# Half of one weight load moved from ScalarE's queue to SyncE's, in a GEGLU feed-forward kernel

## The chip, the core and the metric

The kernel runs on one core of a Trainium2 chip. The core has five engines with their own instruction streams: TensorE (PE, matrix products; its weight loads are listed as PEld), VectorE (DVE), ScalarE (ACT), GpSimd (POOL) and SyncE (SP). Loads and stores are issued by an engine into its queue, and all queues share the core's 16 DMA engines. The metric is device time in microseconds (us): the median of several runs. A profile is one execution, and has a time of its own.

## The reference

```python
def _gelu(x):
    return jax.nn.gelu(x, approximate=True)

# B, S, D, F = 32, 32, 1024, 3584; all inputs bf16
def reference(x, w_gate, w_up, w_down):
    return (_gelu(x @ w_gate) * (x @ w_up)) @ w_down
```

x is 1024 tokens by D = 1024; w_gate and w_up are 1024 by 3584, w_down is 3584 by 1024.

## The kernel before

Each of the two stages of products is computed as a 2x2 block product with seven multiplications instead of eight, at the price of sums of blocks on VectorE, GpSimd and ScalarE.

In the first stage the left matrix is made of w_gate and w_up: for each of the 28 blocks of 128 columns of F (block i), a11 and a12 are the first and second half of D of w_gate's columns, a21 and a22 those of w_up's. The right matrix is x transposed: B11 and B21 are the first and second half of D for tokens 0 to 511, B12 and B22 the same for tokens 512 to 1023. A half of D is four slices of 128 (KH = 4), so one product of two blocks is four matmuls of 128x128 by 128x512. The first product is a11 by B11, the second a12 by B21, added in the same PSUM bank; the fourth to seventh and the third use sums (S1 to S4 of weights, T1 to T4 of x), which are kept in a 4-byte type.

The order of the program is written out by hand. Its start is this. SyncE loads B11 with a transposing DMA (L131) while TensorE runs ten matmuls on constants (L137). ScalarE waits for the second of them and then issues w_gate's tiles (L141 to L145): a tile holds two blocks (256 columns, all of D, 512 KB), and its first half is what a11 reads, its second half what a12 reads. They are issued in this order: tile 0's first half in two pieces of 128 KB, the first halves of tiles 1, 2 and 3 (256 KB each), tile 0's second half. After the ninth constant matmul ScalarE writes a few values into B21 (L147), and this write holds back SyncE's second transposing load, B21 (L149); this is "x's second half". Behind it on SyncE's queue follow the second half of tile 2 (L150), w_up's first 256 columns (L151), the second half of tile 3 (L152), tile 4 (L153), the transposing load of the whole other half of the tokens, xt1 (L154), tile 5 in two halves (L155, L156) and w_up's next 256 columns (L157). Tiles 4 and 5 live in a part of the buffer gT that is not needed yet, so the profile calls them gT. Every load of w_gate is issued by line 86, every load of w_up by line 93, so that in the profile they carry those lines.

TensorE computes the first products of blocks 0 and 1 interleaved (L279), then those of blocks 2 to 7 (L282), then the second products of blocks 0 to 7 (L284), then both products of blocks 8 and 9 (tile 4), the first product of block 10 (tile 5), and from there the products with sums. All their matmuls are on line 195. ScalarE evicts each first product (L212) and applies the GELU to each finished gate block (L219). After the first products of blocks 0 and 1 have been evicted, ScalarE issues the second half of tile 1 (L280).

VectorE's first sums wait for w_up's first load; its T sums (L166) wait for xt1. From about 35 us on the loop runs over the remaining blocks, loading w_gate and w_up a few blocks ahead. The second stage (line 398) multiplies with w_down and stores from line 408 on.

The load helper takes a queue and a range of slices; dt counts the eight slices of D:

Of the kernel before, what the change touches and what calls it, by code (L numbers as in the profile page):

```python
# [12 lines left out]
def kernel(  # L13
# [18 lines left out]
    nc = tc.nc  # L32
# [10 lines left out]
    DT = D // P  # L43
    KH = DT // 2
# [38 lines left out]
    def load_gate(c, queue, lo=0, hi=DT):  # L83
        if c not in WG:
            WG[c] = gw.tile([P, DT, 2 * P], bf16, name="gw", tag="gw")
        queue.dma_start(
            out=WG[c][:, lo:hi, :], in_=wg_r[:, lo:hi, 2 * c * P : (2 * c + 2) * P]
        )

    def load_up(c, lo=0, hi=4):  # L90
        if c not in WU:
            WU[c] = uw.tile([P, DT, 4 * P], bf16, name="uw", tag="uw")
        nc.sync.dma_start(
            out=WU[c][:, :, lo * P : hi * P],
            in_=wu_r[:, :, (4 * c + lo) * P : (4 * c + hi) * P],
        )
# [33 lines left out]
    with tc.manual_schedule():  # L130
# [5 lines left out]
        for n in range(NWARM):  # L136
# [9 lines left out]
            if n == 8:  # L146
                nc.scalar.activation(B21[:, 0, 0:8], table, ACT.Copy)  # L147
                nc.scalar.activation(table, ones[:, 0:8], ACT.Gelu_apprx_tanh)
        nc.sync.dma_start_transpose(out=B21, in_=xf[0:NB, KH * P : D])  # L149
        load_gate(2, nc.sync, KH, DT)  # L150
        load_up(0, 0, 2)  # L151
        load_gate(3, nc.sync, KH, DT)  # L152
# [51 lines left out]
        def first_products(*blocks, cuts=(0, KH)):  # L204
            for i in blocks:
                A[i] = psum_p("a") if 4 <= i < 8 else psum_q("a")
            pair_product([A[i] for i in blocks], [a11(i) for i in blocks], B11, True, cuts)
            for i in blocks:
                if i % 2 == 0:
                    pool, tag = (xpool, "e1") if i == LEAD - 2 else (ring, "ring")  # L210
                    E1[i // 2] = pool.tile([P, 2, NB], fp32, name="e1", tag=tag)
                nc.scalar.activation(E1[i // 2][:, i % 2, :], A[i], ACT.Copy)  # L212
# [64 lines left out]
        t_sum("T3", B22, B12)  # L277
        t_sum("T4", B21, T["T2"])
        first_products(0, 1, cuts=(0, 2, KH))  # L279
        load_gate(1, nc.scalar, KH, DT)  # L280
        for n in range(2, 8):
            first_products(n)  # L282
        for n in range(8):
# [259 lines left out]
```

## Time and profile before

| what | value |
|---|---|
| median of 3 runs | 275.44 us (275.4 to 275.57) |
| profiled execution, its own time | 275.76 us |
| span of the profiled execution | 273.9 us |
| granted TensorE clock | 1.0 |
| VectorE, ScalarE, GpSimd busy | 189.2, 139.7, 87.2 us |
| HBM read, written | 22.02, 2.10 MB |
| SyncE's queue (q1) | 37680 packets, 24.51 MB |
| ScalarE's queue (q10) | 3328 packets, 1.70 MB |

The span is from the first to the last instruction; the rest of the execution's time (1.86 us) lies around it. Times in the chain of waits and in the timeline count from the start of the span. A row of the timeline has the start, the length, engine, line, operation, what is written from what, and how many instructions; in brackets stands how long the engine was idle before and what ended it. An engine named with a q (SPq, ACTq) is its queue, and the length there is that of the issue. A DMA's landing is when its completion is seen.

### The profile page before, as it was taken

How to read it: one execution, taken by the hardware profiler on the slowest of the kernel's cores; microseconds unless marked ns; L12 is line 12 of the kernel's file. 1: busy time of each engine (PE TensorE's matmuls, PEld its weight loads, DVE VectorE, ACT ScalarE, POOL GpSimd, SP SyncE). 2: the span in 40 equal slices, each digit the busy share in tenths (PEclk: the TensorE clock that was granted, in tenths of full speed). 3: DMA queues.
4: the chain of work that ended last, by engine and by line, in shares of the span. 5: the costliest groups of instructions: out<-in, count | busy, mean ns of one | idle time of the engine just before them, and what ended most of it. 6: DMA issues, size and time to landing. Idle time of an engine off the chain costs nothing.

```text
span 273.9 us, 3338 instructions
## 1 busy us (share of the span) xinstructions
PE 268.7 (98%) x1172; PEld 189.4 (69%) x1186; DVE 189.2 (69%) x226; ACT 139.7 (51%) x240; POOL 87.2 (32%) x81
## 2 busy tenths in 40 slices
PE   8999999999999999999999999999999999999995
PEld 2445677778777787776877768764447888888883
DVE  0078885866658666586665866769994999999900
ACT  4778665566565665666655666531100072860311
POOL 0000075745557455584555845600000000000000
PEclk9999999999999999999999999999999999999999
DMA  7999402153300034216360202369602000000321
GB/s 185 277 288 247 154 1 77 52 180 110 121 2 0 0 103 130 77 35 196 96 213 0 77 5 74 107 190 334 214 0 77 2 0 1 0 2 0 116 77 38
DMA packets 41024, 26.42 MB, mean 96 GB/s; under 512 B 9264, under 2 KB 41008, under 8 KB 41008
## 3 DMA queue, kind: packets, MB, share of 16 engines
q1 hardware_dynamic: 37680, 24.51, 30.5%
q10 hardware_dynamic: 3328, 1.70, 2.3%
q8 instruction: 9, 0.15, 0.2%
q14 instruction: 7, 0.06, 0.1%
HBM read 22.02 MB, written 2.10 MB: 88 GB/s over the span
## 4 chain that ended last, share of the span: by engine, by line
PE 94%; DMA 4%; ACT 1%; issue 0%
PE x L195 19%; PE x L398 18%; PE y L115 18%; PE a L195 15%; PE y L398 9%; PE x L115 9%; PE z L398 4%; DMA xt<-in_x_dram 3%; DMA gw<-in_w_gate_dram 1%; PE y L195 1%; ACT L139 0%; ACT o_sb L510 0%
## 5 line engine op out<-in xcount | busy, mean ns | idle before, releaser
L195 PE MATMUL x<-T,s 128*128 128x512 f32 x224 | 63.4, 407 | 0.0
L195 PEld LDWEIGHTS x<-T,s 128*128 128x128 f32 x224 | 41.7, 188 | 10.9 <-ACT e L242 0.3
L195 PE MATMUL a<-xt,gw 128*128 128x512 bf16 x182 | 44.1, 380 | 1.1 <-DMA xt<-in_x_dram 0.3
L259 DVE TENSOR_TENSOR u<-y,e 128x512 bf16<-128x512 f32 x28 | 19.3, 691 | 31.8 <-ACT e L257 30.9
L184 POOL TENSOR_TENSOR s<-gw,s 128x512 fp32r<-128x512 bf16 x22 | 26.0, 1182 | 47.6 <-PE y L115 46.9
L180 DVE TENSOR_TENSOR s<-s,gw 128x512 fp32r<-128x512 f32 x24 | 34.9, 1456 | 0.0
L195 PEld LDWEIGHTS <-gw 128*128 128x128 bf16 x192 | 17.1, 98 | 24.8 <-issue 5.2
L266 ACT ACTIVATE gl<-h 128x512 bf16<-128x512 bf16 x28 | 17.7, 631 | 27.5 <-DVE h L264 27.5
L246 DVE TENSOR_TENSOR gT<-gl,x 128x512 bf16<-128x512 bf16 x28 | 19.2, 686 | 17.9 <-PE x L115 17.9
L115 PE MATMUL x<-T,c 128*128 128x512 f32 x112 | 30.3, 392 | 0.0
L115 PE MATMUL y<-B,s 128*128 128x512 f32 x112 | 30.2, 391 | 0.0
L175 POOL TENSOR_TENSOR s<-uw 128x512 fp32r<-128x512 bf16 x25 | 29.1, 1165 | 0.0
L115 PE MATMUL y<-T,s 128*128 128x512 f32 x104 | 27.8, 389 | 0.0
L398 PE MATMUL x<-tc,sc 128*128 128x512 f32 x112 | 25.7, 389 | 0.0
L257 ACT ACTIVATE e<-x 128x512 f32<-128x512 f32 x28 | 16.7, 600 | 16.0 <-PE x L195 16.0
L176 POOL TENSOR_TENSOR s<-gw,uw 128x512 fp32r<-128x512 bf16 x21 | 24.5, 1167 | 0.0
L115 PEld LDWEIGHTS y<-B,s 128*128 128x128 f32 x112 | 21.0, 188 | 4.8
L212 ACT ACTIVATE e<-a 128x512 f32<-128x512 f32 x28 | 16.6, 597 | 15.2 <-PE a L195 15.2
L115 PEld LDWEIGHTS x<-T,c 128*128 128x128 f32 x112 | 20.9, 188 | 4.8 <-ACT e L257 0.4
L398 PEld LDWEIGHTS x<-tc,sc 128*128 128x128 f32 x112 | 21.0, 188 | 4.4
L115 PEld LDWEIGHTS y<-T,s 128*128 128x128 f32 x104 | 19.5, 188 | 4.1
L219 ACT ACTIVATE gl<-a 128x512 bf16<-128x512 f32 x28 | 16.7, 597 | 7.1 <-PE a L195 7.0
(58 smaller groups left out, 342.0 us busy)
## 6 DMA issues: line engine op xcount, KB each, us to landing
uw<-in_w_up_dram SPq DMA_DIRECT2D x6, 1024.0 KB, 6.4
gw<-in_w_gate_dram SPq DMA_DIRECT2D x8, 512.0 KB, 4.0
v<-in_w_down_dram SPq DMA_DIRECT2D x5, 512.0 KB, 3.8
v<-in_w_down_dram SPq DMA_DIRECT2D x4, 640.0 KB, 8.1
v<-in_w_down_dram SPq DMA_DIRECT2D x8, 256.0 KB, 4.2
out_dram<-o_sb SPq DMA_DIRECT2D x15, 128.0 KB, 1.7
gw<-in_w_gate_dram ACTq DMA_DIRECT2D x5, 256.0 KB, 5.0
uw<-in_w_up_dram SPq DMA_DIRECT2D x2, 512.0 KB, 5.4
```

Of the source, the lines that this page charges most:

```text
L115: nc.tensor.matmul(ps, lhsT=lhs[:, k, :], rhs=rhs[:, k, :], start=(first and k == 0), stop=(k == KH - 1), skip_group_check=True,)
L175: engine.tensor_tensor(S1[i], a21(i), a22(i), ALU.add)
L176: engine.tensor_tensor(S3[i], a11(i), a21(i), ALU.subtract)
L180: nc.vector.tensor_tensor(S2[i], S1[i], a11(i), ALU.subtract)
L184: engine.tensor_tensor(S4[i], a12(i), S2[i], ALU.subtract)
L195: nc.tensor.matmul(p, lhsT=l[:, k, :], rhs=rhs[:, k, :], start=(first and k == 0), stop=(k == KH - 1), skip_group_check=True,)
L219: nc.scalar.activation(GL[i // 2][:, i % 2, :], A[i], ACT.Gelu_apprx_tanh)
L246: nc.vector.tensor_tensor(gT[:, i, 0:NB], GL[i // 2][:, i % 2, :], X[i], ALU.mult)
L257: nc.scalar.activation(e3, X[i], ACT.Copy)
L259: nc.vector.tensor_tensor(U1[i], Y[i], e3, ALU.add)
L266: nc.scalar.activation(G1[i], h1, ACT.Gelu_apprx_tanh)
L398: nc.tensor.matmul(ps, lhsT=lhs[:, i, t * P : (t + 1) * P], rhs=rhs[:, i, :], start=(first and j == 0 and i == 0), stop=(last and j == JF ...
```

## The change

Before, ScalarE's load at L280 brought slices 4 to 7 of D of w_gate's tile 1 (256 KB). Now it brings slices 4 and 5 (128 KB), and a new load on SyncE's queue, between B21 and the second half of tile 2, brings slices 6 and 7 (128 KB). Nothing else differs.

```diff
         nc.sync.dma_start_transpose(out=B21, in_=xf[0:NB, KH * P : D])
+        load_gate(1, nc.sync, KH + 2, DT)
         load_gate(2, nc.sync, KH, DT)
         load_up(0, 0, 2)
         load_gate(3, nc.sync, KH, DT)
...
         first_products(0, 1, cuts=(0, 2, KH))
-        load_gate(1, nc.scalar, KH, DT)
+        load_gate(1, nc.scalar, KH, KH + 2)
         for n in range(2, 8):
             first_products(n)
```

Slices 4 and 5 are read by the first two matmuls of each second product of blocks 2 and 3, slices 6 and 7 by the last two.

## The prediction

> **What bounds the kernel now.** I read the page first (busy times, the chain that ended last), then the chain in order of time, then the first 24 us of the timeline, then what each DMA queue moved in short stretches.
>
> ```profile
> PE 268.7 (98%) x1172; PEld 189.4 (69%) x1186; DVE 189.2 (69%) x226; ACT 139.7 (51%) x240; POOL 87.2 (32%) x81
> PE 94%; DMA 4%; ACT 1%; issue 0%
> ```
>
> TensorE is busy for 98% of the span and is 94% of the chain. Work off TensorE can be worth only what TensorE waits for. The chain in order of time has its DMA share at the start:
>
> ```profile
> 1.83 3.54 DMA gw<-in_w_gate_dram
> 5.37 0.05 issue
> 5.41 0.26 PE a L195
> 5.67 7.18 DMA xt<-in_x_dram
> 12.86 0.14 issue
> ```
>
> (Columns: start, length, what.) x's second half (B21, L149) is issued at 5.67 and lands at 12.86; TensorE starts on it at 12.99. Behind that the chain is TensorE alone, but for its last 0.6 us. The timeline of TensorE there, cut to 12.1 to 13.3 us:
>
> ```profile
> 11.90 0.81 PE L195 MATMUL a<-xt,gw 128*128 128x512 bf16 x3
> 12.99 0.59 PE L195 MATMUL a<-xt,gw 128*128 128x512 bf16 x2 [0.28 <-DMA xt<-in_x_dram]
> ```
>
> The bracket says 0.28 us idle, but ends of matmuls are modelled and overlap, so I go by starts. Three matmuls from 11.90, the last lasting 0.38, put the last start at 11.90 + 0.81 - 0.38 = 12.33. A step is 0.216 us (a row below: 20 matmuls in 4.48 us, (4.48 - 0.38) / 19). The next was due at 12.55 and came at 12.99: **0.44 us are lost here**, and this is the most the change can win. From landing to start it took 0.13, so x would have to land by 12.42 to win it all.
>
> Why does x land at 12.86? What the queues moved (q1 is SyncE's, q10 ScalarE's), first from 9.5 to 11.05 us, then from 11.05 to 11.8:
>
> ```profile
> q1 hardware_dynamic: 1531, 0.39, 112.4%
> q10 hardware_dynamic: 18, 0.01, 2.0%
> ```
>
> ```profile
> DMA packets 535, 0.25 MB, mean 340 GB/s; under 512 B 39, under 2 KB 535, under 8 KB 535
> q10 hardware_dynamic: 506, 0.25, 111.8%
> q1 hardware_dynamic: 29, 0.00, 3.0%
> ```
>
> (Columns: packets, MB, share.) In the first stretch SyncE's queue moves x's 256-byte packets. In the second it moves no data (29 small packets), and ScalarE's queue moves 0.25 MB: w_gate tile 1's second half, the 256 KB load that the change splits. Then SyncE's queue goes on: 0.27 MB from 11.8 to 12.8. So x's data are read by about 11.05, and its landing comes 1.8 us later. I take it that x's completion stands behind that 0.75 us of ScalarE's load. For comparison, the third transpose (L154) is issued at 12.46, takes 9.0 us to land (21.4), and its 256-byte packets end at 20.95: there, with nothing on ScalarE's queue, the lag is about 0.5 us.
>
> **The change part by part.**
>
> 1. ScalarE's load shrinks from 256 to 128 KB. Its issue took 0.37 us at 7.54; the seven issues there, the two of 128 KB (L141, L142) among them, took 0.37 to 0.64 us. So it costs ScalarE between 0 and 0.27 us, taken as 0: ScalarE waits 0.25 us for TensorE before its eviction at 8.43, and that idle covers it; were it gone, the evictions of blocks 2 to 7 would be 0.27 us late, and the first of their PSUM banks is next written by the second product of block 2, at 14.7, six us on. On the DMA engines half of 0.75 us goes from between x's data and x's landing: **0.38 us earlier**, 12.48. TensorE starts at 12.48 + 0.13 = 12.61 and not at 12.99: -0.38. Bounds: 0 (the order of the two is chance or the lag is x's own) and -0.44 (x early enough to win all).
>
> 2. SyncE issues one load more, between L149 and the load of tile 2 (L150). The 256 KB load there took 0.58 us of the queue; the 128 KB rows say 0.43. So tile 2, w_up's first half (L151), tile 3, tile 4 (L153), the transpose of xt1 (L154), tile 5's two halves and w_up's second half can all be issued 0.4 to 0.6 us later. The data are another matter: from 11.8 to 20.9 us the engines moved 2.62 MB at 287 GB/s with hardly a break, and each load's data ran 1 to 6 us behind its issue. The bytes up to each of those loads are the same as before (128 KB change queues, none is added), so I take 0 for their landing; the upper end is 0.58. Issue of the xt1 transpose lasts 6.84 us (12.46 to 19.30), which is the queue being full (L131's transpose of half the bytes took 1.42), so a start 0.58 later can end at the same 19.3.
>
> 3. The moved 128 KB themselves. They run behind x on SyncE's queue, where tile 2's second half ran before: that one was issued at 9.70 and landed 3.8 us later, 13.5. They are needed by the third matmul of block 2 of the second products, 10 steps after the new start: 12.61 + 2.16 = 14.8. Cover 1.3 us, cost 0. TensorE gets one more semaphore to look at there, at weight loads that run ahead; 0, at most the 0.05 of an "issue" piece.
>
> 4. What is late next. With TensorE 0.38 earlier, each later load has 0.38 less room. Tile 2: lands 13.5, needed at 12.99 + 16 steps = 16.4. Tile 4: 11.49 + 6.6 = 18.1, weight load at 19.68. xt1: VectorE starts its T sums at 21.52, the fourth is ready at 24.02 and wanted by the seventh of the eight y products, 1.4 us after their start at 24.02. These have 1 to 3 us. **Tile 5's first half does not.** The two rows of blocks 8, 9 and 10 and the row of the issue:
>
> ```profile
> 19.68 4.20 PEld L195 LDWEIGHTS <-gT 128*128 128x128 bf16 x20
> 19.89 4.48 PE L195 MATMUL a<-xt,gT 128*128 128x512 bf16 x20
> ```
>
> ```profile
> L86 SPq DMA_DIRECT2D gT<-in_w_gate_dram x1: 582/582/582, 19.3 to 19.3; - x1
> DMA to landing us min/median/max: 3.7/3.7/3.7
> ```
>
> Sixteen steps are tile 4's (blocks 8 and 9, both halves); the seventeenth is block 10, tile 5: weight load at 19.68 + 16 x 0.216 = 23.13, matmul at 23.34. Tile 5's first half is issued at 19.34 and lands at 23.05. From landing to weight load was 0.04 at the start of the kernel (5.37 to 5.41), so the room is 0.04 us. If TensorE comes 0.38 early it waits there: the weight load goes at 23.09, its matmul right with it (both stood at 5.41 in the first wait, so the load is not hidden), 23.10 in place of 23.34. Of 0.38 about **0.25 us is kept**. After that the rest follows TensorE, whose chain has no other wait until the end.
>
> Sum: -0.38 + 0.13 = -0.25 us. The profiled execution is 275.76 (span 273.9 and 1.86 around it): it would be 275.51. The median of the runs is 0.32 below that execution, 275.44; the same step gives **275.19**.
>
> **The rivals.**
>
> A. Nothing is won: 275.44, 0.1 either way. x's lag is its own (a transposing load that needs longer to finish), or the 128 KB that stay are still enough to hold it: landing above 12.8. For it: the packets alone do not say which of the 1.8 us are waiting; the second transpose is the only one that runs with ScalarE's loads ahead of it and behind it. Against it: 0.5 us of lag at xt1. In the Trainium skill, "DMA: Bandwidth & Descriptors", section "Issuing engines are not separate DMA queues", it says that DMAs of all issuing engines run on the same 16 engines and interleave, and that a second issuing engine saves only the issue time. By that rule alone the move would be worth 0 here and the time 275.44; the trace agrees on the shared engines (340 GB/s in turn, not together), but shows the two queues running one after the other at 11.05, and then the order decides.
>
> B. Slower: SyncE's added issue of 0.58 us goes through to tile 5's first half, because its issue stands behind xt1's, which is counted from 12.46. Then it lands at 23.63, the weight load goes at 23.67, the matmul at 23.68 in place of 23.34: +0.34, 275.78, whatever x won. It decides from a landing later than 23.05 + 0.25 = 23.30. For it: the room is 0.04 us today. Against it: xt1's data start some 5 us after its issue, so the queue is full and an issue is not what they wait for.
>
> C. The whole 0.44, 275.00: x lands before 12.42 and tile 5's first half by 22.65, since the queue behind x gets going earlier. For it: from 20.95 to 23.1 us the engines move only 263 GB/s, with breaks. Against it: the bytes ahead of it are the same.
>
> **How the numbers follow.** Forecast (0.15 to 0.38 won) 0.48; A 0.22; B 0.16; C 0.08; something unseen 0.06. About 0.2%, 0.55 us, is what a measurement of this kernel can tell from no change. The forecast, A, C and most of B lie within it. Faster by more than that would need more than the 0.44 lost at 12.55: 0.05, out of the unseen and of C. Slower by more needs tile 5 over 0.8 us late, or a wait that I do not see: 0.12, out of B and the unseen. So same is 0.83. Range: from C's 275.00 to B's 275.78, each widened by half the spread of the runs (0.08): 274.92 to 275.86. The forecast's own range is 275.06 to 275.29.
>
> **What would show it.** x's load landing 12.4 to 12.5 and the idle before the second products gone or under 0.1; SyncE's queue without data for 0.4 and not 0.75 us near 11.1; a new wait for tile 5's first half near 23.1 of about 0.1 us; xt1 landing at 21.4 as before. x landing at 12.8 again shows A; tile 5 landing after 23.3 shows B. The prediction is wrong if TensorE waits for tile 1's, 2's or 3's second halves between 12.6 and 19, or if T1 is late at 24.

## The result, and the profile after

The changed kernel takes 276.05 us (median of 13 runs, 275.52 to 276.75), the kernel before, run beside it, 275.51 us (275.15 to 275.77). The ratio is 1.0021, with a 95% interval of 1.0013 to 1.0028: slower, by 0.54 us, about the size that was named as what a measurement can tell; the interval leaves out no change. The forecast was 275.19, and the time lies above the stated range.

The profiled execution of the changed kernel took 276.05 us with a span of 274.3. TensorE's busy time on its page, and the chain that ended last by engine:

```profile
PE 268.5 (98%) x1172; PEld 189.6 (69%) x1186; DVE 189.2 (69%) x226; ACT 139.7 (51%) x240; POOL 87.1 (32%) x81
PE 82%; DMA 8%; SPq 6%; ACT 1%; issue 1%; DVE 0%; ACTq 0%
```

The work is the same; the span is longer by a wait. The chain's larger share of DMA and of SyncE's queue has two parts. One is that wait, below. The other, 5.7% of the span, leads through w_down's loads between 177 and 197 us; TensorE sat idle for none of them, they only landed close to their use. The timeline of TensorE in the first 25 us (start, length, line, operation, count, and in brackets the idle time before):

```profile
5.79 14.05 PE L196 MATMUL a<-xt,gw 128*128 128x512 bf16 x63 [0.59 <-DMA gw<-in_w_gate_dram]
19.68 3.62 PE L196 MATMUL a<-xt,gT 128*128 128x512 bf16 x16
23.70 1.04 PE L196 MATMUL a<-xt,gT 128*128 128x512 bf16 x4 [0.41 <-DMA gT<-in_w_gate_dram]
```

The first row runs through from 5.79 over the place where the kernel before had its wait for x: x's second half lands at 12.23 instead of 12.86, and nothing waits for it. The third row is the new wait: block 10's first product starts at 23.70, 0.57 us after its turn (19.68 and 16 steps of 0.216); in the execution of before it starts at 23.35, without a wait. Behind it nothing more is lost: from 24.3 to 270 us TensorE is busy for 245.04 of 245.70 us here, and for the same 245.04 in a second profile of the kernel before. The chain of waits after, in order of time, shows what stands behind it:

```profile
13.10 7.11 SPq L155
20.25 3.41 DMA gT<-in_w_gate_dram
23.66 0.05 issue
23.70 1.04 PE a L196 x4
```

SyncE's issue of the xt1 transpose (13.10, it was 12.46) lasts until 20.2, tile 5's first half is issued at 20.25 (it was 19.34) and lands at 23.66 (23.05). xt1 itself lands at 22.26 and not at 21.43. From its issue to its landing it takes no longer than before (3.7):

```profile
L86 SPq DMA_DIRECT2D gT<-in_w_gate_dram x1: 582/582/582, 20.2 to 20.2; - x1
DMA to landing us min/median/max: 3.4/3.4/3.4
```

Why that late? Not from the bytes, which are the same. The mean rate of the DMA engines by stretches of 1 us, first in the kernel before, then in the changed one (the columns are the stretch, its length, the busy time and number of instructions of PE, PEld, DVE, ACT and POOL, the granted TensorE clock, and last, what matters here, the DMA engines' busy share and GB/s):

```profile
11.00:12.00 1.00, 1.00 (x6) 0.49 (x5) 0.00 (x0) 0.71 (x2) 0.00 (x0) 1.00 1.16 340
12.00:13.00 1.00, 0.72 (x5) 0.14 (x4) 0.00 (x0) 0.73 (x2) 0.00 (x0) 1.00 1.22 264
...
17.00:18.00 1.00, 1.00 (x7) 0.44 (x5) 0.96 (x3) 0.73 (x2) 0.00 (x0) 1.00 1.25 279
18.00:19.00 1.00, 1.00 (x6) 0.45 (x5) 1.00 (x2) 0.73 (x3) 0.00 (x0) 1.00 1.28 290
```

```profile
11.00:12.00 1.00, 1.00 (x6) 0.48 (x5) 0.00 (x0) 0.60 (x1) 0.00 (x0) 1.00 0.95 243
12.00:13.00 1.00, 1.00 (x7) 0.41 (x6) 0.00 (x0) 0.63 (x2) 0.00 (x0) 1.00 0.89 242
...
17.00:18.00 1.00, 1.00 (x7) 0.44 (x5) 1.00 (x2) 0.62 (x2) 0.00 (x0) 1.00 1.72 224
18.00:19.00 1.00, 1.00 (x6) 0.44 (x5) 0.97 (x3) 0.85 (x2) 0.00 (x0) 1.00 0.79 155
```

Two stretches at a low rate, called pauses or lulls here, are new: one at 11 to 13 us, right behind x, and a deeper one at 17 to 19, where the transpose of xt1 begins (290 GB/s became 155). From the end of x's packets to the end of xt1's it took 9.85 us before and 10.71 after, for the same 2793 KB. The first pause alone costs little of that: from the end of x's packets to 16.5 us the engines moved 1.59 MB at 294 GB/s before and 1.56 MB at 285 GB/s after, a difference worth under 0.2 us. The other 0.7 us go between 17 and 18.6.

A load gives 16 completions, whose times the trace has. Of w_up's first load they come within 0.11 us in the kernel before, and spread over 1.31 us in the changed one. I call this spread "out of step"; the trace doesn't name the engine of a packet, so it is read off these times alone. It is not carried over from the start of the kernel: the load of tile 3's first half spreads over 0.71 us in the kernel before and over 0.51 in the changed one.

The packets of xt1's transpose show what the second pause is. A usual one takes 0.02 us. In the kernel before the longest takes 0.04; the first starts at 17.27, and the last packet of the load ahead (tile 4) ends at 17.31. In the changed kernel the first starts at 17.01, but tile 4's last packet ends at 18.11, and some 20 of xt1's packets stand for up to 1.04 us and end together at 18.5, after which the full rate is there.

### The profile page after: what moved, and what is told of

It is laid out like the page before. It is cut to its first block, busy times and chain, and to the rows that moved or that the text cites. A ratio compares the mean times of both kernels' runs of the same rounds, so it can differ in the third digit from the quotient of the medians.

```text
span 274.3 us, 3341 instructions
## 1 busy us (share of the span) xinstructions
PE 268.5 (98%) x1172; PEld 189.6 (69%) x1186; DVE 189.2 (69%) x226; ACT 139.7 (51%) x240; POOL 87.1 (32%) x81
## 4 chain that ended last, share of the span: by engine, by line
PE 82%; DMA 8%; SPq 6%; ACT 1%; issue 1%; DVE 0%; ACTq 0%
PE x L196 18%; PE y L115 16%; PE x L399 14%; PE a L196 12%; PE y L399 9%; PE x L115 9%; DMA v<-in_w_down_dram 6%; PE z L399 4%; SPq L155 3%; DMA gw<-in_w_gate_dram 1%; DMA gT<-in_w_gate_dram 1%; SPq L86 1%; SPq L363 1%; SPq L370 1%; PE y L196 1%
```

## The experiments

Two theories were set against each other at first. "Issue": SyncE's additional issue pushes back everything behind it, rival B of the prediction. "Skew": the engines come out of step, and the transpose waits for the last of them. All runs were made beside the kernel before (its median was 275.51 to 275.59 in each group). For each run its median is given, and its ratio to the kernel before with the 95% interval.

**All 256 KB on SyncE's queue.**

```diff
         nc.sync.dma_start_transpose(out=B21, in_=xf[0:NB, KH * P : D])
+        load_gate(1, nc.sync, KH, DT)
...
-        load_gate(1, nc.scalar, KH, DT)
```

> All 256 KB of tile 1's second half go over SyncE's queue behind x, none over ScalarE's. Two theories of why tile 5 lands 0.6 us later in the changed kernel. 'Issue': SyncE's one more issue (0.6 us) delays the xt1 transpose and what is issued behind it; SyncE has the same number of issues here as in the changed kernel, so tile 5 is issued near 20.2, its weight load goes near 23.7, and the time is that of the changed kernel, 276.0 to 276.1. 'Skew': the 128 KB load brings the 16 DMA engines out of step, and the transpose, which starts at full rate only when the last of them is through, loses about 0.8 us between 17.3 and 18.5; with a load of 256 KB there is no such lull, tile 5 lands near 23.05 and the time is 275.2 to 275.3. Under both x lands at or before 12.3.

276.57 us, ratio 1.0031 (1.002 to 1.0043). x lands earlier still, at 11.51, tile 5 at 24.26. The pause ahead of xt1 is deeper:

```profile
17.00:18.00 1.00, 1.00 (x6) 0.48 (x5) 1.00 (x2) 0.60 (x1) 0.00 (x0) 1.00 1.80 264
18.00:19.00 1.00, 1.00 (x7) 0.46 (x5) 0.96 (x3) 0.95 (x2) 0.00 (x0) 1.00 0.77 76
```

Neither expectation held. A small load is not needed for it; and with as many issues of SyncE's as in the changed kernel the time is 0.5 us above that one's.

**One issue more behind x, without bytes.**

```diff
         nc.sync.dma_start_transpose(out=B21, in_=xf[0:NB, KH * P : D])
+        nc.sync.dma_start(out=spare, in_=wg_r[:, 0, 0:8])
```

> The kernel before with one more issue on SyncE's queue behind x that moves 2 KB into a tile that nobody reads; ScalarE's load stays whole. Issue: tile 5 lands 0.4 to 0.6 us later, at 23.5 to 23.65, x lands at 12.86 as before, and the time is 0.15 to 0.35 us above the kernel before, 275.65 to 275.85. Skew: nothing of size moves, no lull ahead of the transpose, the time is that of before, 275.5.

275.67 us, 1.0006 (0.9998 to 1.0015): no difference that can be told, and so the time doesn't choose between the two. Tile 5 does: it lands at 22.96, far from the 23.5 of "issue". The spread is 0.42 us and the transfer from x to xt1 0.35 us longer than its bytes ask for: a little of the effect, which this time hides in the slack.

**ScalarE's load in two, both on ScalarE's queue.**

```diff
-        load_gate(1, nc.scalar, KH, DT)
+        load_gate(1, nc.scalar, KH, KH + 2)
+        load_gate(1, nc.scalar, KH + 2, DT)
```

> ScalarE's load is split into two loads of 128 KB, both on ScalarE's queue; SyncE's queue is as before. Issue: time of before, 275.5, x lands near 12.86, tile 5 near 23.05. Skew, if it is the small load as such: a lull of 0.5 us or more ahead of the xt1 transpose near 17 to 18.5, tile 5 lands at 23.5 or later, the time is 275.8 or more.

275.76 us, 1.0009 (1.0 to 1.0018). x lands at 12.68, tile 5 at 22.74, no pause. Splitting as such does not bring the engines out of step; whether it costs the 0.17 us of the median can't be told.

**Tile 5's first half ahead of xt1**, in the changed kernel.

```diff
+        load_gate(5, nc.sync, 0, KH)
         nc.sync.dma_start_transpose(out=xt1, in_=xf[NB:N, :])
-        load_gate(5, nc.sync, 0, KH)
```

> The changed kernel with tile 5's first half issued ahead of the xt1 transpose. Under both theories tile 5 lands by 20 and the wait at 23.7 is gone; what is left is x's earlier landing, up to 0.44 us. xt1 lands 0.9 us later than in the changed kernel, near 23.1: T1's sums then end 0.3 to 0.5 us after the y products want them. If that wait is under 0.2 us the time is 275.2 to 275.4; if xt1 is late by its whole 0.9 us, 275.6 to 275.9.

276.46 us, 1.0028 (1.0017 to 1.0039): worse than either expected case. Tile 5 lands at 19.69, and the wait for it is gone (block 10 starts at 23.27), but xt1 lands at 23.23, and the y products now wait for T1's four sums in turn:

```profile
PEld y L196 <- DVE T L167: 1.2, 4, 0.3
```

They cost about 0.5 us (the next product starts 3.18 us after block 10 in place of 2.70). A later part of the loss, about 0.3 us, was not followed up.

**One issue more right ahead of xt1**, in the kernel before.

```diff
+        nc.sync.dma_start(out=spare, in_=wg_r[:, 0, 0:8])
         nc.sync.dma_start_transpose(out=xt1, in_=xf[NB:N, :])
```

> The kernel before with one more issue on SyncE's queue that moves 2 KB into a tile that nobody reads, this time right ahead of the xt1 transpose, so that only xt1 and what follows it are issued later. Issue: xt1 and tile 5 are 0.4 to 0.6 us later, tile 5 lands near 23.5, time 275.7 to 275.9. Skew: xt1's data are not waiting for their issue; no lull of size ahead of them, tile 5 lands at 22.8 to 23.2, time 275.4 to 275.7.

275.69 us, 1.0009 (1.0 to 1.0018). The time doesn't choose here either. xt1 is issued at 13.82, 1.4 us later than in the first profile of the kernel before, and tile 5 lands at 22.80. So the issue theory falls for xt1 and what follows it: a load that has five us of others ahead of it doesn't notice a late issue.

**The 128 KB behind tile 2's second half**, in the changed kernel.

```diff
         load_gate(2, nc.sync, KH, DT)
+        load_gate(1, nc.sync, KH + 2, DT)
```

> The changed kernel with the 128 KB on SyncE's queue behind tile 2's second half and not ahead of it. Theory 'hole': a load behind the transpose has its first data 1.7 to 2.0 us after its issue; 128 KB on SyncE's queue last 0.45 us, and the next load is issued 0.63 later, so the engines run dry near 11.8 to 12.2, come out of step there, and lose it again at the xt1 transpose. With 256 KB first the next load is there in time: completions of a load come within 0.3 us of each other, the lull ahead of xt1 is under 0.4 us, tile 5 lands at 23.2 or before, x still lands at 12.2 to 12.5, time 275.2 to 275.5. If the small load as such, wherever it stands, or ScalarE's smaller load brings the engines out of step: lull of 0.8 us or more, tile 5 at 23.6, time 275.9 to 276.1.

276.05 us, 1.0021 (1.0012 to 1.003). Here "hole" was wrong: a load of 256 KB first leaves the engines as much out of step (spread 1.82 us), and tile 5 lands at 23.67.

**Both kernels profiled once more.**

> The kernel before, profiled once more, to see which of its times repeat. All theories: x lands 12.4 to 12.9, no lull ahead of xt1, tile 5 lands within 0.3 us of 23.05.

> The changed kernel, profiled once more. Skew and hole: the lull ahead of xt1 (0.5 to 1.3 us at low rate between 17 and 19) and the wait of TensorE for tile 5 near 23.1 to 23.7 are there again. If they were chance, tile 5 lands near 23.05 and the span is under 273.8.

The changed kernel repeats: spread 0.84, tile 5 at 23.89, span 274.6, and the wait:

```profile
23.93 1.04 PE L196 MATMUL a<-xt,gT 128*128 128x512 bf16 x4 [0.44 <-DMA gT<-in_w_gate_dram]
```

The kernel before does not repeat in one point:

```profile
5.63 14.24 PE L195 MATMUL a<-xt,gw 128*128 128x512 bf16 x63 [0.44 <-DMA gw<-in_w_gate_dram]
19.71 4.48 PE L195 MATMUL a<-xt,gT 128*128 128x512 bf16 x20
```

There is no wait for x in it. x lands at 12.56, and TensorE, which began 0.22 us later than in the first profile (5.63, not 5.41), is there later than that. The 0.44 us that the forecast meant to win were the size of one execution. In the seven profiles with 256 KB on ScalarE's queue, this one and those of the experiments among them, TensorE's wait for x is 0 to 0.44 us by the starts of matmuls (0.37 in the run with two loads on ScalarE's queue); in those with 128 KB or none there is no wait. Nor does TensorE wait for tile 5 here, which lands at 22.78.

**ScalarE's queue filled up again.** A third theory, "feed", asks when the engines reach SyncE's first plain load behind x, counted from its issue: they stay in step only if that load was issued some 2.0 us before they come to it.

```diff
         load_gate(1, nc.scalar, KH, KH + 2)
+        nc.scalar.dma_start(
+            out=gT[:, 0, 0:NB].rearrange("p (a f) -> p a f", f=2 * P),
+            in_=wg_r[:, KH + 2 : DT, 2 * P : 4 * P],
+        )
```

> The changed kernel with ScalarE's queue filled up to 256 KB again: behind its 128 KB it loads 128 KB more (slices 6 and 7 of tile 1 a second time, into a part of gT that is written over later). SyncE's queue is as in the changed kernel. Theory 'feed': SyncE's first plain load behind the transpose goes in step only if the engines come to it some 2.0 us or more after its issue; with 256 KB on ScalarE's queue they come to it near 11.6 to 11.8, 2.0 after the issue, as in the kernel before. Then completions come close together, there is no lull above 0.4 us ahead of xt1, and tile 5 lands at 23.1 to 23.4 although 128 KB (0.45 us) more are moved; x lands at 12.4 to 12.9; time 275.5 to 275.8. Theory 'SyncE': it is the small load, or the one load more, on SyncE's queue behind x; then the lull stays and tile 5 lands at 24.1 or later, time 276.3 or more.

SyncE's queue is that of the changed kernel, 128 KB more are moved, and the pause is gone:

```profile
17.00:18.00 1.00, 1.00 (x7) 0.47 (x5) 0.96 (x3) 0.69 (x2) 0.00 (x0) 1.00 1.25 276
18.00:19.00 1.00, 1.00 (x7) 0.41 (x5) 1.00 (x3) 1.00 (x3) 0.00 (x0) 1.00 1.28 290
```

The spread is 0.19 us, and tile 5 lands at 23.33, earlier than in the changed kernel (23.66 and 23.89). So SyncE's additional load alone doesn't make the pause. The time is 276.05 us, 1.0018 (1.0008 to 1.0027), 0.25 above what was expected and no better than the changed kernel's: TensorE still waits for tile 5, 0.49 us by the starts of matmuls. That this is the price of the repeated 128 KB (about 0.45 us of transfer) fits, but is not shown; "feed" is borne out by the landings and not by the time.

**ScalarE's load cut, nothing on SyncE's queue.**

```diff
-        load_gate(1, nc.scalar, KH, DT)
+        load_gate(1, nc.scalar, KH, KH + 2)
...
     def a12(i):
-        return block(WG, 2, i, 1)
+        return block(WG, 2, i + 2 if i in (2, 3) else i, 1)
```

> The kernel before with ScalarE's load cut to 128 KB and nothing put on SyncE's queue: slices 6 and 7 of tile 1 are not loaded, and the second products and S4 of blocks 2 and 3 use tile 2's second half of w_gate in place of tile 1's. SyncE's issues are those of before. Feed: the engines come to tile 2's second half near 11.3, 1.7 to 1.8 after its issue, fall out of step, the lull of 0.6 us or more ahead of xt1 is there, and tile 5 lands at 22.9 or later although 0.45 us less is moved. SyncE: no lull, tile 5 lands 0.45 us earlier than in the kernel before, near 22.4, and no slower than before. x lands at 12.0 to 12.4 under both.

This kernel leaves out 128 KB of w_gate. 275.22 us, 0.9991 (0.9982 to 1.0001). Mixed: tile 5 lands at 22.47, near what "SyncE" gave, but 0.45 us less is moved and only 0.3 of it is won against 22.78; spread 0.45, excess 0.29 us (the time lost between x and the end of xt1; the table below has it for all). The effect is there at a third of its size.

**Two issues more behind x, ScalarE's load whole.**

```diff
         nc.sync.dma_start_transpose(out=B21, in_=xf[0:NB, KH * P : D])
+        nc.sync.dma_start(out=spare, in_=wg_r[:, 0, 0:8])
+        nc.sync.dma_start(out=spare2, in_=wg_r[:, 0, 0:8])
```

> The kernel before, ScalarE's load whole, with two more issues of 2 KB each on SyncE's queue behind x, so that tile 2's second half is issued 1.2 us later, near 10.7, while the engines still come to it near 11.5. Feed: the engines come 0.8 us after the issue, run dry and fall out of step: completions of w_up's first load are spread over 0.8 us or more (0.11 in the kernel before, 0.42 with one extra issue, 0.8 to 1.3 in the changed kernel), the transpose loses 0.8 us or more in all, tile 5 lands at 23.6 or later, time 276.0 or more, though no byte has changed its queue. If ScalarE's 256 KB as such keep the engines in step: spread under 0.4 us; the pause near 11.5 to 12.5 alone can cost up to 1 us.

275.95 us, 1.0017 (1.0007 to 1.0026). No load of the kernel changed its queue or its size, but tile 2's second half and the loads behind it are issued later (10.47 and not 9.45), and the median is 0.44 us above the kernel before, where the change costs 0.54. The pause behind x is there:

```profile
11.00:12.00 1.00, 1.00 (x6) 0.46 (x5) 0.00 (x0) 0.73 (x2) 0.00 (x0) 1.00 0.97 206
12.00:13.00 1.00, 1.00 (x5) 0.32 (x4) 0.00 (x0) 0.73 (x2) 0.00 (x0) 1.00 0.84 242
```

The 2 KB as such are not what it costs: ahead of xt1 such a load left an excess of 0.05 us. The sizes are under the expected ones (spread 0.61, tile 5 at 23.31, time 275.95 and not 276.0). The profiled execution took 275.57 us, the least of the ten, so its trace shows less of the loss than the median has.

**Tile 5's first half in two loads**, in the changed kernel.

```diff
-        load_gate(5, nc.sync, 0, KH)
+        load_gate(5, nc.sync, 0, 2)
+        load_gate(5, nc.sync, 2, KH)
```

> The changed kernel with tile 5's first half loaded as two loads of two slices each, behind xt1 as before. If the wait for tile 5 is the whole loss of the change: the first two slices land 0.4 us before the whole did, near 23.2 to 23.4, the other two are wanted 0.43 us later, the wait near 23.7 shrinks by 0.3 to 0.45 us and the time is 275.55 to 275.8. If the loss is elsewhere too (T sums, a later wait): 276.0.

275.69 us, 1.0008 (0.9999 to 1.0018): two thirds of the loss are gone, and the rest can't be told from nothing. The engines are nearly as late as in the changed kernel (xt1's packets end at 21.65, there at 21.73), but the first two slices land at 23.03, and block 10 starts in its turn:

```profile
19.62 4.53 PE L197 MATMUL a<-xt,gT 128*128 128x512 bf16 x20
23.80 2.21 PE L197 MATMUL y<-T,s 128*128 128x512 f32 x8
```

So the wait for tile 5 was the loss, or most of it. No version that loads everything was found to beat the kernel before.

**All profiles in one table.** "Lead": from the issue of SyncE's first plain load of size behind x to its first packet. "Excess": the time from the end of x's packets to the end of xt1's, less the KB moved at the kernel before's 284 KB per us. "Spread": of the completions of w_up's first load. "Longest": the longest packet of xt1's transpose. The last two columns are the profiled execution's own time and the median. us.

| kernel | lead | excess | spread | longest | tile 5 lands | block 10 starts | its time | median |
|---|---|---|---|---|---|---|---|---|
| before, first profile | 2.08 | 0.02 | 0.11 | 0.04 | 23.05 | 23.35 | 275.76 | 275.51 |
| before, second profile | 2.10 | -0.01 | 0.09 | 0.03 | 22.78 | 23.17 | 275.53 | |
| two loads on ScalarE's queue | 2.13 | -0.01 | 0.20 | 0.04 | 22.74 | 23.17 | 275.59 | 275.76 |
| an issue ahead of xt1 | 2.10 | 0.05 | 0.09 | 0.04 | 22.80 | 23.05 | 275.51 | 275.69 |
| ScalarE's queue filled up | 2.11 | -0.01 | 0.19 | 0.05 | 23.33 | 23.38 | 275.89 | 276.05 |
| ScalarE's load cut | 1.71 | 0.29 | 0.45 | 0.42 | 22.47 | 23.22 | 275.59 | 275.22 |
| an issue behind x | 1.52 | 0.35 | 0.42 | 0.37 | 22.96 | 23.01 | 275.44 | 275.67 |
| two issues behind x | 1.13 | 0.67 | 0.61 | 0.53 | 23.31 | 23.35 | 275.57 | 275.95 |
| changed, tile 5 in two | 1.72 | 0.74 | 0.49 | 0.88 | 23.03 | 23.08 | 275.69 | 275.69 |
| changed, first profile | 1.69 | 0.87 | 1.31 | 1.04 | 23.66 | 23.70 | 276.05 | 276.05 |
| changed, second profile | 1.67 | 0.96 | 0.84 | 1.24 | 23.89 | 23.94 | 276.36 | |
| changed, tile 5 ahead of xt1 | 1.69 | 1.02 | 1.48 | 1.27 | 19.69 | 23.27 | 276.47 | 276.46 |
| changed, behind tile 2 | 1.73 | 1.16 | 1.82 | 1.48 | 23.67 | 23.72 | 276.14 | 276.05 |
| all on SyncE's queue | 1.32 | 1.33 | 1.80 | 1.48 | 24.26 | 24.31 | 276.65 | 276.57 |

Five profiles with a lead of 2.08 or more have an excess of 0.05 at most. Nine with 1.73 or less have 0.29 to 1.33. There is none in between. Below the step the lead doesn't set the size: the spread and the longest packet of xt1 go with it better.

The table also shows that the loss goes through block 10: but for the run with tile 5 ahead of xt1, a profiled execution's time less block 10's start is 252.2 to 252.6 in every row. Single executions differ by as much as some of the effects, so a row's landings belong to its own time and not to its median.

## Why the prediction was wrong

**x lands earlier (step 1): the mechanism was right.** x's completion does come behind what ScalarE's queue still holds. It landed at 12.86 and 12.56 with 256 KB there, at 12.23 and 12.32 with 128, and at 11.51 with none; the other runs lie at 12.4 to 12.7 with 256 KB and at 12.0 to 12.3 with 128. The forecast was 12.48.

**What it is worth (the 0.44 us lost): mis-sized.** The second profile of the kernel before shows no wait for x. So the gain was between 0 and 0.44, by the execution; I took one execution's wait for the kernel's. Its first matmul at 5.41 was the earliest but one of all profiles (5.40 to 5.79), and its x the latest.

**The landings behind x (step 2): the step that failed.** It said that the bytes up to each load are the same, "so I take 0 for their landing". The bytes were the same, but the engines stopped moving them at the full rate: 0.87 and 0.96 us are lost between x and the end of xt1, most of it where xt1 begins and its first packets stand until tile 4's last has ended. The time counted on "with hardly a break", a property that the trace of before had because ScalarE's 256 KB kept the engines at work until SyncE's next load had been issued for 2.1 us. Taking half of that away shortened the lead to 1.7. That the lead matters is shown from both sides: later issues with the same bytes bring an excess (0.35 and 0.67), and with ScalarE's queue filled up again the excess is gone. The shorter load on ScalarE's queue alone brings 0.29, SyncE's additional load alone none; only the two together bring the change's 0.9 (one profile for each of these runs). The upper end of 0.58 was too small as well: tile 5 lands 0.6 and 0.8 us later than in the first profile of before, 0.9 and 1.1 later than in the second.

**What is late next (step 4): right place.** Tile 5 was named, with a room of 0.04 us in the first profile (0.14 in the second, counted the same way), and that is where the time went, as block 10's starts and the run with tile 5 in two loads show.

**Rival B: right in place and sign, wrong in mechanism.** It priced +0.34 at 23.68; the trace has 23.70, but the second profile 23.94, and the medians are 0.54 apart: the near hit is luck. It put the delay on SyncE's issues standing in line, and the run with an issue ahead of xt1 shows that these do not reach xt1. An issue counts only at the loads that the engines come to soon after it, as the runs with one and two issues behind x show.

**Rival A and the rule quoted for it**, that a second issuing engine saves only issue time (the Trainium skill, "DMA: Bandwidth & Descriptors", "Issuing engines are not separate DMA queues"): the shared engines are borne out, but here where a load is queued cost them 0.9 us, so the rule doesn't carry as an estimate. Rival C's 0.44 did not come.

**What stays open.** Why the engines come out of step below a lead of about 2 us, and what sets by how much, is not shown: the trace has no engine for a packet, and between 1.73 and 2.08 nothing was run. That the transpose of xt1 starts at full rate only when the last engine is through is seen in the packets: in each of the nine profiles with an excess 16 to 22 packets of xt1 stand, and end together about 0.4 us after the last packet of the load ahead has ended; in the other five no packet of xt1 takes more than 0.05 us. Why they stand is not shown. Where the 0.18 us went by which the run with tile 5 in two loads lies above the kernel before, if they are real, is open too.

## What to carry to other kernels

Where a queue of loads runs without a break, ask what covers the time between a load's issue and its first packet; a transfer on another queue may be that cover, and to shrink it can cost more than its bytes are worth. Look up the load that lands just in time some ten us later before winning tenths at the front, and split it if it is the one that is waited for. A wait of a few tenths in one profile should be seen in a second one before it is priced.

## What was not expected of the hardware

Where the engines came to SyncE's plain load 1.13 to 1.73 us after its issue, its first packet went at once, but not the rest: in the run with all on SyncE's queue, whose load was issued at 9.61, the engines moved 63 GB/s from 11.0 to 11.5 us, and with two issues behind x, where it was issued at 10.47, 77 GB/s from 11.6 to 12.2. The price came six us later, at the next transpose: its first packets stood for up to 1.48 us, until the last one of the load ahead had ended. Until then, while the engines are out of step, the rate is higher for a while (336 GB/s from 14 to 15 us in the changed kernel, against 290 in step), which gives back a part.
